# A decode block streamed through one core: 24 VectorE instructions joined or moved, and w2 loaded in four pieces

## The chip, the core and the metric

The kernel runs on one core of a Trainium2 chip. The core has TensorE (matrix products into PSUM), VectorE, ScalarE and GpSimd (elementwise work and reductions), and SyncE, which here issues every transfer between main memory (HBM) and SBUF. The five engines run their own instruction streams and wait for one another by semaphores. The metric is the device time of one execution in microseconds; lower is better.

## The reference

One token goes through a transformer block with adaptive layernorm. D is 640, there are 32 heads of 192, the cache holds 8192 positions, and the hidden layer has 1536. Everything is float32.

```python
mod = (silu(c) @ w_mod).reshape(1, 6, 1, 640)
sa, ca, ga, sb, cb, gb = (mod[:, i] for i in range(6))
h = layernorm(x) * (1 + ca) + sa
q = (h @ wq).reshape(1, 1, 32, 192).transpose(0, 2, 1, 3)
p = softmax(einsum("bhqd,bhkd->bhqk", q, k_cache) * 192 ** -0.5)
o = einsum("bhqk,bhkd->bhqd", p, v_cache)          # heads joined: 6144
x = x + ga * (o @ wo)
h = layernorm(x) * (1 + cb) + sb
r = maximum(h @ w1 + b1, 0)
x = x + gb * ((r * r) @ w2 + b2)
```

The caches are 201 MB each. Every byte of them is used once, so nearly all of the 452 MB that the kernel reads are cache.

## The kernel before

**The stream.** `plan()` cuts the work into 53 chunks. A chunk holds, for each of the 128 partitions, a row of key positions, a row of value units, and now and then a block of wq (for the next 512 columns of the query) or of wo (for the next pair of heads). A chunk has at most 16128 floats a partition, about 8 MB in all, and lies in one of three slots (`strm`, `slot`). SyncE issues `load(n + 3)` at the end of chunk n's part of the program; that transfer waits until every engine is through with the slot, and lies then in the queue behind what was issued before it. Behind the last chunk the same three slots take wm1 (the modulation weights for ga, sb, cb and gb), w1 and w2. The transfer of w2 is cut by `W2_CUT` into pieces, and each piece has a semaphore of its own. The products that read a piece wait for that piece. w2 has 12 blocks, each of 640 columns on 128 partitions (328 kB).

**The head of the program.** First comes wm0 (the weights for sa and ca, the first block of wq, x, c and the biases, in one transfer), and beside it wm0x, six small transfers into a part of the same slot that VectorE and GpSimd have filled with zeros. From these the program makes silu(c), the first two modulations, the first layernorm (`layernorm`, whose sums over partitions go through TensorE by `total`, a product with a tile of ones) and the first 512 columns of the query (`query`). Only then can VectorE begin on chunk 0.

**A chunk.** TensorE sums values weighted with p (`values`, line 331). VectorE multiplies the keys with the query (`multiply`, line 282). GpSimd adds the two halves of some of the products, and VectorE reduces the rest (`scores`, line 290). When a head's keys are through, `softmax` takes the maximum through a transpose on TensorE and lets ScalarE do the exponential. For each pair of heads `inverse` gives one over the sum on each partition, `evict` and `turn` bring the output of the heads into a column form (oT), and `attend` multiplies it by that pair's rows of wo, adding up in PSUM (att_a). The order of all this is the order of the code: there is no scheduler, and each engine runs its part in the order written.

**The tail.** After the last chunk the last pair is turned and attended, `mod` and `gate` make the last four modulations, `gather` brings the sum of the attention together, and the second layernorm gives h. The product with w1 goes to PSUM as ps_f. After it come two products into a bank that nobody reads (`ps_idle`). VectorE adds the bias, applies relu and the square, and transposes the result into fT. The product with w2 goes into ps_y, block by block (line 480), 4 matmuls a block, one for each quarter of the columns. VectorE multiplies by gb, adds x, and SyncE stores 640 floats.

The profile records a float32 matmul as two rows, so a block of w2 shows as 8 rows of TensorE.

Of the kernel before, what the change touches and what calls it, by code (L numbers as in the profile page):

```python
# [8 lines left out]
F32 = mybir.dt.float32  # L9
AF = mybir.ActivationFunctionType  # L10
ALU = mybir.AluOpType
AX = mybir.AxisListType

P = 128
D = 640
# [5 lines left out]
DG = D // G  # L21
FG = FF // G
KB = DG // 32
# [4 lines left out]
NV = DH // ED  # L28
# [17 lines left out]
LEAD_FROM = 1300  # L46
LEAD = 120
W1_CUT = (3 * FF, KB * FF)
W2_CUT = (6 * D, 10 * D, 12 * D)
WM_CUT = (KB * D + 9 * D, KB * D + 15 * D)  # L50
IDLE = 2
EPS = 1e-5
# [41 lines left out]
def block_kernel(ctx: ExitStack, tc: tile.TileContext, kv, wm0, wm0x, wm1, w1, w2, out):  # L94
    nc = tc.nc
    const = ctx.enter_context(tc.tile_pool(name="const", bufs=1))
# [5 lines left out]
    def slot(name):  # L102
        return strm.tile([P, SLOT], F32, tag="slot", name=name, bufs=3)
# [2 lines left out]
    ident = const.tile([P, P], F32, name="ident")  # L106
    make_identity(nc, ident)
    ones = const.tile([P, P], F32, name="ones")
    nc.vector.memset(ones, 1.0)

    mask = const.tile([P, E], F32, name="mask")
    nc.vector.tensor_reduce(mask, ident.rearrange("p (g e c) -> p e g c", g=G, e=E), axis=AX.XY, op=ALU.add)
    sel = const.tile([P, 1], F32, name="sel")
    nc.vector.tensor_reduce(sel, ident.rearrange("p (g c) -> p c g", g=G)[:, 0], axis=AX.X, op=ALU.add)
    eps_t = const.tile([P, 1], F32, name="eps_t")
    nc.vector.memset(eps_t, EPS)

    wm0_t = slot("wm0_t")
    wm0x_t = wm0_t[:64, SLOT - SX * WX:]
# [10 lines left out]
    x_c, c_c, bbc = small[:, :KB], small[:, KB:2 * KB + SX], small[:, 2 * KB + SX:]  # L130

    def columns(src, n, name, pool=const, **how):

        t = pool.tile([P, n // 32, 32], F32, name=name, **how)
        nc.vector.transpose(t.rearrange("p b r -> p (b r)"), src)
        return t
# [9 lines left out]
    def total(src, name):  # L146

        n = src.shape[1]
        ps = psum.tile([P, 512], F32, tag="sm", name="ps_" + name, bufs=2)
        nc.tensor.matmul(ps[:, :n], ones, src, start=True, stop=True)  # L150
        return ps[:, :n]

    def layernorm(x, copies, scale1, shift, name, between=lambda: None):

        n = x.shape[1]
        s = const.tile([P, 1], F32, name=name + "_s")
        nc.vector.tensor_reduce(s, x, axis=AX.X, op=ALU.add)
        m = const.tile([P, 1], F32, name=name + "_m")
        between()
        tm = total(s, name + "_tm")  # L160
        between()
        nc.vector.tensor_scalar(m, tm, 1.0 / (copies * D), None, op0=ALU.mult)
        xm = const.tile([P, n], F32, name=name + "_xm")
        nc.vector.tensor_scalar(xm, x, m, None, op0=ALU.subtract)
        sq = const.tile([P, n], F32, name=name + "_sq")
        ss = const.tile([P, 1], F32, name=name + "_ss")
        nc.vector.scalar_tensor_tensor(sq, xm, 1.0, xm, op0=ALU.mult, op1=ALU.mult, accum_out=ss)
        sd = const.tile([P, 1], F32, name=name + "_sd")
        nc.scalar.activation(sd, total(ss, name + "_tv"), AF.Sqrt, bias=eps_t, scale=1.0 / (copies * D))
        between()  # L170
        rs = const.tile([P, 1], F32, name=name + "_rs")
        nc.vector.reciprocal(rs, sd)
        h = const.tile([P, n], F32, name=name + "_h")
        nc.vector.scalar_tensor_tensor(h, xm, rs, scale1(), op0=ALU.mult, op1=ALU.mult)
        nc.vector.tensor_add(h, h, shift())
        return h


# [6 lines left out]
    mods = const.tile([P, 6, DG], F32, name="mods")  # L185
# [25 lines left out]
    def gate(m, w, steps):  # L211

        ps = psum.tile([P, 512], F32, tag="q", name=f"ps_mod{m}", bufs=2)
        b = 0
        for n in steps:
            for b in range(b, b + n):
                for k in range(2):
                    nc.tensor.matmul(ps[64 * k:64 * (k + 1), :2 * DG], e[:, b:b + 1].to_broadcast([P, 64]),
                                     w[:, b, 2 * DG * k:2 * DG * (k + 1)], start=(b == 0), stop=(b == KB - 1))
            b += 1  # L220
            yield
        for g in range(G):
            r = slice(32 * g, 32 * (g + 1))
            nc.scalar.activation(mods[r, m], ps[r, DG * (g % 2):DG * (g % 2 + 1)], AF.Copy)
        yield
# [4 lines left out]
    def load(n):  # L230
# [5 lines left out]
        else:  # L236
            name, src, cuts = (("wm1_t", wm1, WM_CUT), ("w1_t", w1, W1_CUT), ("w2_t", w2, W2_CUT))[n - len(PLAN)]
            chunk_t[name] = slot(name)
# [8 lines left out]
    load(1)  # L247
    mod(0, 2, wm0_t, wm0x_t)
    ma = columns(mods[:, 0:2].rearrange("p m n -> p (m n)"), 2 * DG, "ma")
    ca1 = const.tile([P, KB], F32, name="ca1")  # L250

    def scale_a():
        nc.vector.tensor_scalar(ca1, ma[:, KB:, 0], 1.0, None, op0=ALU.add)
        return ca1

    h1 = layernorm(x_c, 1, scale_a, lambda: ma[:, :KB, 0], "ln1")
    qb = const.tile([P, RING], F32, name="qb")

    def query(u, w):
        w = w.rearrange("p (b n) -> p b n", b=KB)  # L260
        ps = psum.tile([P, 512], F32, tag="q", name=f"ps_q{u}", bufs=2)
        for b in range(KB):
            nc.tensor.matmul(ps, h1[:, b:b + 1].to_broadcast([P, P]), w[:, b], start=(b == 0), stop=(b == KB - 1))  # L263
        nc.scalar.activation(qb[:, QC * u % RING:QC * u % RING + QC], ps, AF.Copy, scale=DH ** -0.5)  # L264


    att_a = psum.tile([P, 512], F32, tag="att", name="att_a")
    att_s = const.tile([P, D], F32, name="att_s")
    nc.vector.memset(att_s, 0.0)
    query(0, wm0_t[:, W0:W0 + WQ])  # L270

    sc = const.tile([P, SRING], F32, name="sc")
# [20 lines left out]
    ri_t, ps_t, sum_t = {}, {}, {}  # L293
# [57 lines left out]
    def turn(i):  # L351
        oT = work.tile([P, NV], F32, tag="oT", name=f"oT{i}")
        nc.vector.tensor_reduce(oT, os_t[i][:, :96].rearrange("p (j r) -> p j r", j=NV), axis=AX.X, op=ALU.add)  # L353
        nc.vector.tensor_scalar(oT, oT, ri_t.pop(i), None, op0=ALU.mult)  # L354
        os_t[i] = oT

    def attend(i, w):
        oT = os_t.pop(i)
        w = w.rearrange("p (j n) -> p j n", j=NV)
        first, last = i == 0, i == NPAIR - 1  # L360
        oW = work.tile([P, NV, 32], F32, tag="oW", name=f"oW{i}")
        nc.scalar.activation(oW, oT[:, :, None].to_broadcast([P, NV, 32]), AF.Copy)  # L362
        for j in range(NV):
            nc.tensor.matmul(att_a[96:, :512], oT[:, j:j + 1].to_broadcast([P, 32]), w[:, j, :512],  # L364
                             start=(first and j == 0), stop=(last and j == NV - 1))
        nc.tensor.matmul(att_a[:96, :NV * (D - 512)], oW.rearrange("p j r -> p (j r)"), w[:, :, 512:],  # L366
                         start=first, stop=last)
# [19 lines left out]
    for n, (kp, nk, vp, nv, extra) in enumerate(PLAN):  # L387
# [5 lines left out]
        for what, k in extra:  # L393
            w = t[:, at:at + EXTRA[what]]
# [10 lines left out]
        if nk:  # L405
            multiply(kt, kp, nk)
            m = nk - POOL * nk // 16
# [10 lines left out]
        for h in evicted:  # L418
            if h % 2:
                turn(h // 2)  # L420
# [11 lines left out]
        if wo_t is not None and n + 1 < len(PLAN):  # L432
            attend(*wo_t)
# [7 lines left out]
    for h in to_evict:  # L441
        evict(h)
    turn(NPAIR - 1)
    attend(*wo_t)
    mod(2, 3, wm1_t[:, KB * D:KB * 4 * D], between=gather)
    x1 = const.tile([P, DG], F32, name="x1")
    nc.vector.tensor_mul(x1, att_t[0][:, :DG], mods[:, 2])
    nc.vector.tensor_add(x1, x1, x_t)

    def scale_b():  # L450
        cb1 = const.tile([P, DG], F32, name="cb1")
        nc.vector.tensor_scalar(cb1, mods[:, 4], 1.0, None, op0=ALU.add)
        return cb1

    last = gate(5, gb_t, (2, 1, 2))
    hT2 = columns(layernorm(x1, 32, scale_b, lambda: mods[:, 3], "ln2", lambda: next(last)), DG, "hT2")
    next(last)

    pf = psum.tile([P, 512], F32, tag="q", name="ps_f", bufs=2)
# [6 lines left out]
        nc.tensor.matmul(idle, ones, w1_t[:, k, :512], start=True, stop=True)  # L466
    f = work.tile([P, FG], F32, name="f", tag="spread", bufs=1)
    nc.vector.tensor_add(f, pf[:, :FG], bbt[:, :FG])
    nc.vector.tensor_scalar(f, f, 0.0, None, op0=ALU.max)
    nc.vector.tensor_mul(f, f, f)  # L470
    fT = columns(f, FG, "fT", work, tag="om", bufs=1)

    gb2 = const.tile([P, DG], F32, name="gb2")
# [63 lines left out]
```

## Time and profile before

| | |
|---|---|
| median of three runs | 1055.33 us |
| lowest and highest | 1055.12, 1056.24 us |
| the profiled execution | 1055.26 us |
| its span, first to last instruction | 1053.5 us |
| HBM read | 451.83 MB |
| VectorE instructions, busy | 429, 831.5 us |
| ScalarE instructions, busy | 122, 43.5 us |
| GpSimd instructions, busy | 58, 189.7 us |
| mean granted TensorE clock | 0.723 of full speed |

The 1.8 us between the execution's time and its span lie around the first and the last instruction. Busy times of different engines overlap and don't add up to the span. In a group's row of the profile the columns are: line, engine, operation, output and inputs with their shape, count, then busy time in us and the mean of one in ns, then the idle time of the engine just before them and what ended it. A line of the chain has a start, a length and what ran. PE stands for TensorE and PEld for its weight load, DVE for VectorE, ACT for ScalarE, POOL for GpSimd, SP for SyncE.

### The profile page before, as it was taken

Reading aid. Unit: us, or ns where it says so; the run is one execution under the profiler, and the core shown is the slowest. Engines: PE = TensorE matmul, PEld = TensorE weight load, DVE = VectorE, ACT = ScalarE, POOL = GpSimd, SP = SyncE. Lnnn points to the kernel's source line nnn. Section 1 sums busy time; section 2 is a strip of 40 time slices with the busy share of each in tenths; the row PEclk is TensorE's granted clock in tenths of the full one; section 3 lists DMA queues with packets and bytes.
Section 4 is the critical chain, followed back from the end, with each engine's and each line's share of the span. In section 5 each row is a group of like instructions: output and inputs, shape, how many; then the busy total and the mean of one; then the engine's idle time right before and its main releaser. Section 6 shows DMA issues by size and latency. Waiting matters only on the chain.

```text
span 1053.5 us, 5195 instructions
## 1 busy us (share of the span) xinstructions
PE 495.3 (47%) x2130; PEld 135.0 (13%) x2130; DVE 831.5 (79%) x429; ACT 43.5 (4%) x122; POOL 189.7 (18%) x58
## 2 busy tenths in 40 slices
PE   3253344465352373435453366245346345445387
PEld 1010011011010010101010011001011011011023
DVE  1899878877959959888697895999888977988822
ACT  1000000000000000000000000000000000000001
POOL 0212121121212201212121121121211211212200
PEclk9676576778675686668667577676777767668689
DMA  9999999999999999999999999999999999999997
GB/s 408 427 432 443 437 438 436 428 430 429 434 436 431 432 431 435 436 430 437 430 427 431 434 445 436 431 427 433 431 432 437 431 434 434 434 436 431 420 426 317
DMA packets 8999, 452.15 MB, mean 429 GB/s; under 512 B 1016, under 2 KB 1020, under 8 KB 1148
## 3 DMA queue, kind: packets, MB, share of 16 engines
q1 hardware_dynamic: 8976, 451.83, 99.3%
q8 instruction: 16, 0.26, 0.1%
q14 instruction: 7, 0.06, 0.0%
HBM read 451.83 MB, written 0.00 MB: 429 GB/s over the span
## 4 chain that ended last, share of the span: by engine, by line
DMA 56%; DVE 31%; PE 11%; ACT 1%; issue 0%; SPq 0%; DVEq 0%
DMA chunk<-in_kv 53%; DVE chunk L282 16%; DVE sc L290 13%; PE ps_o L331 5%; PE att_a L364 2%; DMA w_t<-in_w 2%; PE ps_q L263 2%; DMA wm_t<-in_wm 1%; DVE os L345 1%; DVE om L343 1%; PE att_a L366 0%; ACT p L314 0%; PE ps_mx L306 0%; PE ps_mod L201 0%; PE ps_mod L207 0%
## 5 line engine op out<-in xcount | busy, mean ns | idle before, releaser
L282 DVE TENSOR_TENSOR chunk<-chunk,qb 128x8064 f32<-128x8064 f32 (+19 forms) x81 | 419.7, 5212 | 122.7 <-DMA chunk<-in_kv 118.0
L290 DVE TENSOR_REDUCE sc<-chunk 128x25 f32<-128x4800 f32 (+21 forms) x109 | 333.9, 3097 | 0.4
L409 POOL TENSOR_TENSOR chunk<-chunk 128x1824 f32<-128x1824 f32 (+9 forms) x51 | 187.4, 3674 | 803.8 <-DVE chunk L282 570.3
L331 PE MATMUL ps_o<-chunk,p 128*32 128x512 f32 x1536 | 292.3, 726 | 71.0 <-DMA chunk<-in_kv 61.5
L306 PE MATMUL ps_mx<-ident,mp 128*128 128x128 f32 x32 | 14.3, 447 | 346.4 <-DVE mp L304 346.4
L331 PEld LDWEIGHTS ps_o<-chunk,p 128*32 128x32 f32 x1536 | 66.6, 130 | 270.8 <-issue 184.0
L364 PE MATMUL att_a<-chunk,oT 128*32 128x512 f32 x96 | 68.1, 867 | 42.8 <-DVE oT L354 42.8
L263 PE MATMUL ps_q<-chunk,ln_h 128*128 128x512 f32 x110 | 65.8, 758 | 24.9 <-DMA chunk<-in_kv 24.9
L306 PEld LDWEIGHTS ps_mx<-ident,mp 128*128 128x128 f32 x32 | 5.6, 174 | 376.0 <-DVE mp L304 330.1
L314 ACT ACTIVATE p<-sc,nm 128x256 f32<-128x256 f32 x32 | 16.2, 507 | 648.5 <-DVE nm L308 648.5
L263 PEld LDWEIGHTS ps_q<-chunk,ln_h 128*128 128x128 f32 x110 | 26.4, 251 | 62.7 <-issue 34.5
L343 DVE TENSOR_TENSOR om<-ps_o,mask 96x512 f32<-96x512 f32 x32 | 21.6, 675 | 8.5 <-PE ps_o L331 8.5
L308 DVE TENSOR_REDUCE nm<-ps_mx 128x1 f32<-128x128 f32 x32 | 9.3, 292 | 19.9 <-PE ps_mx L306 19.9
L345 DVE TENSOR_REDUCE os<-om 96x64 f32<-96x512 f32 x32 | 21.8, 682 | 1.1
L364 PEld LDWEIGHTS att_a<-chunk,oT 128*32 128x32 f32 x96 | 12.4, 144 | 80.1 <-DVE oT L354 45.4
L353 DVE TENSOR_REDUCE oT<-ps_oT 128x3 f32<-128x96 f32 x16 | 4.0, 248 | 21.8 <-PE ps_oT L349 21.8
L319 PE MATMUL ps_sum<-ident,wide 128*128 128x128 f32 x16 | 7.5, 467 | 22.4 <-ACT wide L317 22.4
L349 PE MATMUL ps_oT<-ident,os 96*128 96x96 f32 x16 | 5.1, 321 | 25.8 <-DVE os L345 25.8
L201 PE MATMUL ps_mod<-wm_t,silu 128*32 128x480 f32 (+2 forms) x78 | 8.7, 584 | 14.4 <-DVE silu L183 14.4
L366 PE MATMUL att_a<-chunk,oW 128*96 128x384 f32 x32 | 14.8, 545 | 0.0
L264 ACT ACTIVATE qb<-ps_q 128x512 f32<-128x512 f32 x12 | 7.2, 597 | 135.4 <-PE ps_q L263 135.4
L362 ACT ACTIVATE oW<-oT 128x96 f32<-128x96 f32 x16 | 4.5, 280 | 176.5 <-DVE oT L354 176.5
(84 smaller groups left out, 104.8 us busy)
## 6 DMA issues: line engine op xcount, KB each, us to landing
chunk<-in_kv SPq DMA_DIRECT2D x38, 8064.0 KB, 35.1
chunk<-in_kv SPq DMA_DIRECT2D x11, 8000.0 KB, 37.2
chunk<-in_kv SPq DMA_DIRECT2D x2, 7872.0 KB
chunk<-in_kv SPq DMA_DIRECT2D x1, 6144.0 KB, 22.5
wm_t<-in_wm SPq DMA_DIRECT2D x1, 4480.0 KB
wm_t<-in_wm SPq DMA_DIRECT2D x1, 4257.0 KB, 12.5
chunk<-in_kv SPq DMA_DIRECT2D x1, 3264.0 KB
chunk<-in_kv SPq DMA_DIRECT2D x1, 3072.0 KB
```

Of the source, the lines that this page charges most:

```text
L263: nc.tensor.matmul(ps, h1[:, b:b + 1].to_broadcast([P, P]), w[:, b], start=(b == 0), stop=(b == KB - 1))
L282: nc.vector.tensor_mul(pr, pr, q[:, None, :].to_broadcast([P, b - a, DH]))
L290: nc.vector.tensor_reduce(sc[:, a % SRING:a % SRING + b - a], src[:, a - first:b - first], axis=AX.X, op=ALU.add)
L306: nc.tensor.transpose(ps[:, :P], mp.to_broadcast([P, P]), ident)
L308: nc.vector.tensor_reduce(nm, ps[:, :P], axis=AX.X, op=ALU.max, negate=True)
L314: nc.scalar.activation(p, s[:, :, None].to_broadcast([P, NPOS, 32 // E]), AF.Exp, bias=nm, accum_out=sp[:, h % 2:h % 2 + 1])
L331: nc.tensor.matmul(ps_t[h][32 * g:32 * (g + 1)], p[:, E * j:E * (j + 1)].rearrange("p e r -> p (e r)"), t[:, g], start=(j == 0), stop=last)
L343: nc.vector.tensor_mul(om[:n], ps_t.pop(h)[:n].rearrange("p (d e) -> p d e", e=E), mask[:n, None, :].to_broadcast([n, ED, E]))
L345: nc.vector.tensor_reduce(os_[:n, h % 2], om[:n], axis=AX.X, op=ALU.add)
L364: nc.tensor.matmul(att_a[96:, :512], oT[:, j:j + 1].to_broadcast([P, 32]), w[:, j, :512], start=(first and j == 0), stop=(last and j == NV ...
L366: nc.tensor.matmul(att_a[:96, :NV * (D - 512)], oW.rearrange("p j r -> p (j r)"), w[:, :, 512:], start=first, stop=last)
L409: nc.gpsimd.tensor_add(half, half, kt[:, m:, DH // 2:])
```

## The change

Five things are changed, and all values computed stay the same up to rounding.

1. In `turn` the multiplication of oT by one over the softmax sum is taken out (16 VectorE instructions, one for each pair). ScalarE's copy of oT into oW applies it as the copy's scale. The three wide products of `attend` read oW in place of oT, so they too now follow ScalarE's copy.
2. In `layernorm` the mean is no longer scaled by itself: one joined operation subtracts the scaled sum from x. The squares are written into h, which is overwritten later. The factor 1 + scale is multiplied into x minus the mean before the reciprocal of the root, and the last joined operation multiplies by that reciprocal and adds the shift. The instructions `ca1` and `cb1` are gone. Each of the two layernorms has two VectorE instructions fewer.
3. Relu and square are one joined operation.
4. `ones`, `eps_t` and `att_s` are filled by GpSimd in place of VectorE.
5. w2 comes in pieces of 6, 3, 2 and 1 block where it came in 6, 4 and 2.

```diff
-W2_CUT = (6 * D, 10 * D, 12 * D)
+W2_CUT = (6 * D, 9 * D, 11 * D, 12 * D)
...
-    nc.vector.memset(ones, 1.0)
+    nc.gpsimd.memset(ones, 1.0)
...
-    nc.vector.memset(eps_t, EPS)
+    nc.gpsimd.memset(eps_t, EPS)
...
-    def layernorm(x, copies, scale1, shift, name, between=lambda: None):
+    def layernorm(x, copies, scale, shift, name, between=lambda: None):
...
-        m = const.tile([P, 1], F32, name=name + "_m")
         between()
         tm = total(s, name + "_tm")
         between()
-        nc.vector.tensor_scalar(m, tm, 1.0 / (copies * D), None, op0=ALU.mult)
         xm = const.tile([P, n], F32, name=name + "_xm")
-        nc.vector.tensor_scalar(xm, x, m, None, op0=ALU.subtract)
-        sq = const.tile([P, n], F32, name=name + "_sq")
+        nc.vector.scalar_tensor_tensor(xm, tm.to_broadcast([P, n]), -1.0 / (copies * D), x, op0=ALU.mult, op1=ALU.add)
+        h = const.tile([P, n], F32, name=name + "_h")
         ss = const.tile([P, 1], F32, name=name + "_ss")
-        nc.vector.scalar_tensor_tensor(sq, xm, 1.0, xm, op0=ALU.mult, op1=ALU.mult, accum_out=ss)
+        nc.vector.scalar_tensor_tensor(h, xm, 1.0, xm, op0=ALU.mult, op1=ALU.mult, accum_out=ss)
         sd = const.tile([P, 1], F32, name=name + "_sd")
         nc.scalar.activation(sd, total(ss, name + "_tv"), AF.Sqrt, bias=eps_t, scale=1.0 / (copies * D))
         between()
+        nc.vector.scalar_tensor_tensor(xm, scale(), 1.0, xm, op0=ALU.add, op1=ALU.mult)
         rs = const.tile([P, 1], F32, name=name + "_rs")
         nc.vector.reciprocal(rs, sd)
-        h = const.tile([P, n], F32, name=name + "_h")
-        nc.vector.scalar_tensor_tensor(h, xm, rs, scale1(), op0=ALU.mult, op1=ALU.mult)
-        nc.vector.tensor_add(h, h, shift())
+        nc.vector.scalar_tensor_tensor(h, xm, rs, shift(), op0=ALU.mult, op1=ALU.add)
         return h
...
-    nc.vector.memset(att_s, 0.0)
+    nc.gpsimd.memset(att_s, 0.0)
...
-        nc.vector.tensor_scalar(oT, oT, ri_t.pop(i), None, op0=ALU.mult)
...
-        nc.scalar.activation(oW, oT[:, :, None].to_broadcast([P, NV, 32]), AF.Copy)
+        nc.scalar.activation(oW, oT[:, :, None].to_broadcast([P, NV, 32]), AF.Copy, scale=ri_t.pop(i))
         for j in range(NV):
-            nc.tensor.matmul(att_a[96:, :512], oT[:, j:j + 1].to_broadcast([P, 32]), w[:, j, :512],
+            nc.tensor.matmul(att_a[96:, :512], oW[:, j], w[:, j, :512],
                              start=(first and j == 0), stop=(last and j == NV - 1))
...
-    nc.vector.tensor_scalar(f, f, 0.0, None, op0=ALU.max)
-    nc.vector.tensor_mul(f, f, f)
+    nc.vector.scalar_tensor_tensor(f, f, 0.0, f, op0=ALU.max, op1=ALU.mult)
```

Three places show how the instructions stand before and after. In the rows, `x7` counts equal instructions, and the brackets name the engines or transfers whose semaphores an instruction waits for (DMAHW is a transfer's).

The first is ScalarE at the head of the program: silu, then the root of the first layernorm, then the first query and the table for the exponential. Before:

```order
L180 ACT_TABLE_LOAD
L180 ACTIVATE silu<-small 128x12 [waits DVE_49]
L169 ACT_TABLE_LOAD
L169 ACTIVATE ln_sd<-ps_ln_tv,eps_t 128x1 [waits PE_49]
L264 ACTIVATE qb<-ps_q_167 128x512 [waits PE_49]
L314 ACT_TABLE_LOAD
```

And now:

```order
L177 ACT_TABLE_LOAD
L177 ACTIVATE silu<-small 128x12 [waits DVE_49]
L167 ACT_TABLE_LOAD [waits PE_49]
L167 ACTIVATE ln_sd<-ps_ln_tv,eps_t 128x1 [waits Pool_49]
L255 ACTIVATE qb<-ps_q_162 128x512 [waits PE_49]
L305 ACT_TABLE_LOAD
```

The root now waits for GpSimd (eps_t) as well as for TensorE, and the wait for TensorE stands on the table load ahead of it.

The second is TensorE at the end of the program, where w1's product (ps_f), the two unread products and w2's product (ps_y) follow one another. Before:

```order
L462 MATMUL ps_f<-w_t,hT_2153 32x384 [waits DMAHW0_49]
L462 MATMUL ps_f<-w_t,hT_2153 32x384 x7
L466 MATMUL ps_idle<-w_t,ones 128x512 x2
L480 MATMUL ps_y<-w_t,fT 32x160 [waits DVE_49,DMAHW1_49,PE_49,Activation_49]
L480 MATMUL ps_y<-w_t,fT 32x160 x23
L480 MATMUL ps_y<-w_t,fT 32x160 [waits DMAHW2_49]
L480 MATMUL ps_y<-w_t,fT 32x160 x15
L480 MATMUL ps_y<-w_t,fT 32x160 [waits DMAHW3_49]
L480 MATMUL ps_y<-w_t,fT 32x160 x7
```

And now:

```order
L447 MATMUL ps_f<-w_t,hT_2128 32x384 [waits DMAHW0_49]
L447 MATMUL ps_f<-w_t,hT_2128 32x384 x7
L451 MATMUL ps_idle<-w_t,ones 128x512 [waits PE_49]
L451 MATMUL ps_idle<-w_t,ones 128x512
L464 MATMUL ps_y<-w_t,fT 32x160 [waits DVE_49,DMAHW1_49,PE_49,Activation_49]
L464 MATMUL ps_y<-w_t,fT 32x160 x23
L464 MATMUL ps_y<-w_t,fT 32x160 [waits DMAHW2_49]
L464 MATMUL ps_y<-w_t,fT 32x160 x11
L464 MATMUL ps_y<-w_t,fT 32x160 [waits DMAHW3_49]
L464 MATMUL ps_y<-w_t,fT 32x160 x7
L464 MATMUL ps_y<-w_t,fT 32x160 [waits DMAHW4_49]
L464 MATMUL ps_y<-w_t,fT 32x160 x3
```

Behind the last wait for a transfer stand 4 matmuls, where there were 8, and there is one such wait more.

The third is VectorE at the same place, from the second layernorm to fT. Before:

```order
L162 TENSOR_SCALAR ln_m<-ps_ln_tm 128x1 [waits PE_49]
L164 TENSOR_SCALAR ln_xm<-x_2117,ln_m 128x160 [waits DVE_49]
L167 SCALAR_TENSOR_TENSOR ln_sq,ln_ss<-ln_xm 128x160 [waits DVE_49]
L172 RECIPROCAL ln_rs<-ln_sd 128x1 [waits Activation_49]
L452 TENSOR_SCALAR cb_2149<-mods 128x160
L174 SCALAR_TENSOR_TENSOR ln_h<-ln_xm,ln_rs,cb_2149 128x160 [waits DVE_49]
L175 TENSOR_TENSOR ln_h<-ln_h,mods 128x160 [waits DVE_49]
L135 STREAM_TRANSPOSE hT_2153<-ln_h 128x160 [waits DVE_49]
L468 TENSOR_TENSOR f<-ps_f,bbt 128x384 [waits PE_49]
L469 TENSOR_SCALAR f<-f 128x384 [waits DVE_49]
L470 TENSOR_TENSOR f<-f 128x384 [waits DVE_49]
L135 STREAM_TRANSPOSE fT<-f 128x384 [waits DVE_49]
```

And now:

```order
L162 SCALAR_TENSOR_TENSOR ln_xm<-ps_ln_tm,x_2097 128x160 [waits PE_49]
L165 SCALAR_TENSOR_TENSOR ln_h,ln_ss<-ln_xm 128x160 [waits DVE_49]
L169 SCALAR_TENSOR_TENSOR ln_xm<-mods,ln_xm 128x160 [waits DVE_49]
L171 RECIPROCAL ln_rs<-ln_sd 128x1 [waits Activation_49]
L172 SCALAR_TENSOR_TENSOR ln_h<-ln_xm,ln_rs,mods 128x160 [waits DVE_49]
L135 STREAM_TRANSPOSE hT_2128<-ln_h 128x160 [waits DVE_49]
L453 TENSOR_TENSOR f<-ps_f,bbt 128x384 [waits PE_49]
L454 SCALAR_TENSOR_TENSOR f<-f 128x384 [waits DVE_49]
L135 STREAM_TRANSPOSE fT<-f 128x384 [waits DVE_49]
```

The product with 1 + scale (L169) now stands ahead of the instruction that waits for the root, and nine instructions stand where there were twelve.

More of the change, by code (lines that the diff above doesn't have):

```diff
@@ L249, in block_kernel @@
     ma = columns(mods[:, 0:2].rearrange("p m n -> p (m n)"), 2 * DG, "ma")
[L250 to L256, printed above, removed]
+    h1 = layernorm(x_c, 1, lambda: ma[:, KB:, 0], lambda: ma[:, :KB, 0], "ln1")
     qb = const.tile([P, RING], F32, name="qb")
@@ L448, in block_kernel @@
     nc.vector.tensor_add(x1, x1, x_t)
[L450 to L453, printed above, removed]
     last = gate(5, gb_t, (2, 1, 2))
-    hT2 = columns(layernorm(x1, 32, scale_b, lambda: mods[:, 3], "ln2", lambda: next(last)), DG, "hT2")
+    hT2 = columns(layernorm(x1, 32, lambda: mods[:, 4], lambda: mods[:, 3], "ln2", lambda: next(last)), DG, "hT2")
     next(last)
```

## The prediction

> **What bounds the kernel now.** I read the page first (shares, slices, queues, chain), then the chain of waits in order of time at both ends, then the timeline of the last 15 us, then the groups by line, and last the windows of half a microsecond for the granted clock.
>
> ```profile
> PE 495.3 (47%) x2130; PEld 135.0 (13%) x2130; DVE 831.5 (79%) x429; ACT 43.5 (4%) x122; POOL 189.7 (18%) x58
> DMA  9999999999999999999999999999999999999997
> q1 hardware_dynamic: 8976, 451.83, 99.3%
> HBM read 451.83 MB, written 0.00 MB: 429 GB/s over the span
> DMA 56%; DVE 31%; PE 11%; ACT 1%; issue 0%; SPq 0%; DVEq 0%
> L282 DVE TENSOR_TENSOR chunk<-chunk,qb 128x8064 f32<-128x8064 f32 (+19 forms) x81 | 419.7, 5212 | 122.7 <-DMA chunk<-in_kv 118.0
> chunk<-in_kv SPq DMA_DIRECT2D x38, 8064.0 KB, 35.1
> ```
>
> VectorE is busy 79% of the span and is named in 31% of the chain, which would make 24 fewer of its instructions look valuable. The other rows say no. The one queue of transfers is busy 99.3% of all 16 engines' time, no slice but the last is under 9 tenths, and VectorE's multiplies stood idle 118.0 us for chunks that had not landed. A typical chunk is 8064 KB, that is 8.26 MB. At the mean 429 GB/s it takes 19.2 us to move, but it lands 35.1 us after its issue. So it sat about 16 us behind the chunk ahead of it. The stream is fed early, and the VectorE pieces in the chain are only the last event before an issue that was itself early. The tightest early issue is chunk 3's:
>
> ```profile
> 0.74 12.50 DMA wm_t<-in_wm
> ...
> 46.97 10.22 DVE sc L290 x2
> ...
> 57.20 30.03 DMA chunk<-in_kv
> ```
>
> It still took 30.03 us, so 10.8 us of it was queueing. VectorE may be that much later there before the stream feels it. The stream itself begins at 0.74 us, with the first load, which waits for nothing.
>
> The end is the stream's end, and what follows it. The first rows are of the chain, the next of the timeline (start, length, and in brackets the idle time before and what ended it), the last of the transfers with their sizes:
>
> ```profile
> 1029.34 19.88 DMA w_t<-in_w
> ...
> 1049.26 0.80 PE ps_y L480 x16
> ...
> 1050.08 0.34 DVE y L483
> ...
> 1044.78 1.84 PE L480 MATMUL ps_y<-w_t,fT 128*32 128x160 f32 x48 [0.95 <-DVE x L475]
> 1047.75 1.29 PE L480 MATMUL ps_y<-w_t,fT 128*32 128x160 f32 x32 [1.13 <-DMA w_t<-in_w]
> 1049.26 0.75 PE L480 MATMUL ps_y<-w_t,fT 128*32 128x160 f32 x16 [0.22 <-DMA w_t<-in_w]
> ...
> w_t<-in_w SPq DMA_DIRECT2D x1, 1280.0 KB
> w_t<-in_w SPq DMA_DIRECT2D x1, 640.0 KB
> ```
>
> The last transfer of w2 was issued at about 1029.3 and landed at 1049.22. TensorE waited for the second and the third piece of w2 (1047.75, 1049.26), so the chain of small operations before it is not last. The third piece is 640 KB (655 KB in thousands) and landed 1.51 us after the second: 434 GB/s, the stream's own pace, 0.75 us a block.
>
> **The change, part by part.**
>
> *w2 in 6, 3, 2, 1 blocks.* This is the one part on the path. The 48, 32 and 16 records (two a matmul) took 1.84, 1.29 and 0.75 us, so eight matmuls more cost 0.55 and 0.54 us: 0.068 us each, over some 0.2 us that every group pays. After the last landing now come 4 matmuls in place of 8: 4 x 0.068 = 0.27 us less. The two-block piece lands at about 1049.22 - 0.75 = 1048.47, and its 0.75 us are over as the last block lands; if it is late by a little, it eats part of the gain. The path gains 0.27 us.
>
> One transfer is added, with 128 packets of 2560 bytes, 8 for each engine. SP issues it at about 1029.7, some 19 us ahead of need. The trace has no packet of that size. From below, the 640 KB piece with 5120-byte packets ran at 434 GB/s, so nothing: 0. From above, the same trace's smallest transfer, the output:
>
> ```profile
> 1052.00:1052.50 0.50, 0.00 (x0) 0.00 (x0) 0.00 (x0) 0.00 (x0) 0.00 (x0) 1.00 0.02 5
> out_y<-y SPq DMA_DIRECT2D x1, 2.5 KB
> ```
>
> A share of 0.02 (0.025 at most) of 16 engines in half a microsecond is 0.2 us for its 4 packets, 0.05 us each, where 640 bytes at 27 GB/s need 0.024: at most 0.03 us extra a packet, 0.2 us for eight. I take 0, since the 5120-byte packets are nearest in size; 0.2 stays for the range. A gain is excluded: the bytes are the same.
>
> The two landings 1.51 us apart leave no room for a time of its own between queued transfers. The Trainium skill, "DMA: Bandwidth & Descriptors", section "Anatomy of one DMA — SWDGE (gpsimd) path", gives each transfer a fixed cost of about 2.0 us beside its bytes, measured on GpSimd's path; by it, if paid in turn, the sum would be -0.27 + 2.0 = +1.7 us.
>
> *The 16 multiplications by the inverse sum (L354).*
>
> ```profile
> L354 DVE TENSOR_SCALAR oT<-oT,r 128x3 f32<-128x3 f32 x16 | 3.7, 228 | 0.6
> L362 ACT ACTIVATE oW<-oT 128x96 f32<-128x96 f32 x16 | 4.5, 280 | 176.5 <-DVE oT L354 176.5
> ```
>
> VectorE is relieved of 16 x 0.228 = 3.7 us (4.1 with the handover). All of it lies in front of waits for chunks, the last pair's in front of w1 and w2: worth 0. For each pair TensorE's three wide products now read ScalarE's copy, so they wait 0.280 us for it where they waited 0.228 for L354: about 0.05 us later, unless the per-partition scale makes the copy dearer (a copy with a scale and one without are not side by side in the trace; anything up to doubling it stays under 0.4 us). Behind them in TensorE's queue are the products with values, and SP's issue of a later chunk waits for the pair's last product: 0.4 us against 10.8 us of queueing. Worth 0.
>
> *The first layernorm.* On its path one VectorE instruction goes ahead of the sum of squares and two behind the root. But ScalarE's root now needs eps_t from GpSimd as well as TensorE's sum; the wait for TensorE stands on the table load ahead of it.
>
> ```profile
> 13.71 1.28 ACT L169 ACT_TABLE_LOAD   x1
> 24.21 0.16 DVE L162 TENSOR_SCALAR ln_m<-ps_ln_tm 128x1 f32<-128x1 f32 x1 [0.47 <-PE ps_ln_tm L150]
> 25.52 0.26 ACT L169 ACTIVATE ln_sd<-ps_ln_tv,eps_t 128x1 f32<-128x1 f32 x1 [10.53 <-PE ps_ln_tv L150]
> 26.34 0.17 DVE L175 TENSOR_TENSOR ln_h<-ln_h,ma 128x5 f32<-128x5 f32 x1
> 33.97 12.96 DVE L282 TENSOR_TENSOR chunk<-chunk,qb 128x12288 f32<-128x12288 f32 x1 [4.70 <-ACT qb L264]
> ```
>
> Before, the load ran at 13.71, long before the root at 25.52. Now it starts at about 25.3: +1.28 us. The joined instructions give back 0.19 (L162 and its handover), 0.19 (the scale of 1 + ca) and 0.26 (L175): 0.64. The query, and with it the first multiply, comes 0.6 us later, at about 34.6. Chunk 3 is issued at 57.8 in place of 57.2, out of 10.8 us of queueing. Worth 0; if the cover were gone, +0.6.
>
> *Memsets to GpSimd.* The two of ones and eps now stand ahead of wm0x's memset on GpSimd, some 0.3 us by its own 128x128 memset (0.20). SP's six small loads and chunk 0 wait for that one, 3.3 to 3.6; they queue behind the first load, which lands at 13.24. The third, att_s, is needed at 1028. GpSimd's first real work is at 47. Worth 0.
>
> *The second layernorm and relu-square.* At about 1035 to 1044, L162 and its handover (0.20) against a costlier joined subtraction, 1 + cb and L175 (0.26 and 0.36) against a product done while the root is awaited, and L469 (0.36 and its handover, 0.39) go: about 1.1 us.
>
> ```profile
> L469 DVE TENSOR_SCALAR f<-f 128x384 f32<-128x384 f32 x1 | 0.4, 360 | 0.0
> L452 DVE TENSOR_SCALAR cb<-mods 128x160 f32<-128x160 f32 x1 | 0.2, 224 | 0.0
> L175 DVE TENSOR_TENSOR ln_h<-ln_h,mods 128x160 f32<-128x160 f32 x1 | 0.3, 325 | 0.0
> L480 PEldq EVENT_SEMAPHORE  x2: 51/51/51, 1044.2 to 1044.7; - x2
> 1043.56 0.58 DVE L135 STREAM_TRANSPOSE fT<-f 128x384 f32<-128x384 f32 x1
> ```
>
> fT was ready at 1044.14, and TensorE's second wait ended at 1044.7: that is w2's first piece (four blocks at 0.75 us ahead of 1047.75 agree). Being 1.1 us earlier only lengthens that wait. Worth 0.
>
> **Sum.** On the profiled execution: 1055.26 - 0.27 + 0 = 1055.0 us (1053.5 of it span, 1.8 around it). The median of the runs before is 1055.33, 0.07 above that execution, so this is also 0.3 us under the median.
>
> **The rivals.**
>
> *The VectorE chain counts.* If the 31% were true limits, all removed work would show: 4.1 us of L354, 1.1 us in the tail, 0.27: 1049.8. For it: the chain's share. Against it: 118.0 us of waiting for chunks, 99.3% on the queue.
>
> *TensorE's clock falls at the end (slower).* With fT up to 1.1 us earlier, TensorE rests longer before w2's first piece. The columns here are the stretch, its length, the busy time of PE, PEld, DVE, ACT and POOL, the granted clock, the share of the transfer engines and GB/s.
>
> ```profile
> 1020.80:1024.20 3.40, 1.27 (x4) 0.47 (x5) 1.84 (x4) 0.28 (x1) 0.00 (x0) 1.00 0.89 381
> 1024.50:1027.50 3.00, 3.00 (x5) 0.35 (x3) 0.00 (x0) 0.00 (x0) 0.00 (x0) 0.50 1.05 441
> 1041.30:1044.70 3.40, 2.53 (x12) 0.68 (x4) 2.58 (x6) 0.00 (x0) 0.00 (x0) 1.00 0.97 401
> ```
>
> After 3.4 us in which TensorE was busy 37%, the granted clock was 0.50 for the next 3 us, although TensorE worked all through them. A stretch of 74% (1041.30 on) kept 1.00. With the change that last stretch holds at most 0.6 us less work: 1.9 of 3.4, 56%, between the two. If the clock falls at 1044.7 and stays down to the end, 48 matmuls at twice 0.068 and the 0.2 take until 1044.75 + 6.7 = 1051.5, where 1049.26 + 0.80 = 1050.06 was: +1.4, or 1056.7 us. It decides from the point where that stretch comes near 37%. The Trainium skill, "TensorE: Matmul & The Clock Gate", section "HAM oscillation — how this bites in real kernels", has the rule that the array must not rest more than about 3.4 us on end. By it a wait of 1.4 us is harmless. The trace's fall, after a stretch that was busy for 37%, is stricter than that rule, so I leave the rival a chance.
>
> *The added transfer costs a time of its own (slower).* A lone small transfer does: the output's was issued from 1050.79 for 0.60 us, and the span ends at 1053.5, 2.1 us behind that.
>
> ```profile
> 1050.79 0.60 SPq L485 DMA_DIRECT2D out_y<-y  x1
> ```
>
> If the fourth piece paid that in turn, behind the third, the end would be 1055.0 + 2.1 = 1057.1. Against it: two queued pieces 1.51 us apart at full pace. The page named above would give 2.0 for the 2.1; the landings here don't bear it out for queued transfers.
>
> *The stream runs slower.* The end hangs on 451.83 MB at 429 GB/s; the three runs before lay from 1055.12 to 1056.24, so one in three stood 0.9 us above the median with nothing changed. That gives 1056.1; twice that excess is 1057.1.
>
> *The change does not do what it says.* The instruction order shows that it does, with the table load's wait as the one thing unsaid: +0.6 us if it counted, 1055.6.
>
> **How the numbers follow.** Forecast 1055.0, by about a microsecond to each side: 0.72. A slower stream: 0.13. The clock: 0.05. The added transfer's own time: 0.03. The table load or another small wait of the head that comes through: 0.02. The VectorE chain: 0.05. A measurement of this kernel can tell about 0.2% from no change, 2.1 us: below 1053.2 or above 1057.4. Faster by more has the VectorE chain alone, 0.05. Slower by more has the far end of the stream's scatter, and a little of the clock and the added transfer on top of it: 0.07. Within it: 0.88. The range starts a microsecond under the forecast, since the scatter seen has only gone up, and ends where the clock rival and most of the stream's scatter lie: 1054.0 to 1056.9.
>
> **What would show it.** Right: the last group of TensorE's L464 starts as w2's last piece lands and is over some 0.5 us later in place of 0.80; SP's issues, the queue's 99% and the landing of w2 stay where they are; VectorE has about 5 us less busy time and as much more waiting for chunks; the first multiply starts at 34 to 35 us, after a table load at about 25. Wrong: VectorE's wait for chunks stays at 118 us while the span shrinks; a granted clock of 0.50 after 1044; the last piece of w2 landing more than 0.2 us later than 1049.2; a slice of the queue under 9 tenths.

## The result, and the profile after

The changed kernel takes 1052.56 us (median; 1052.38 to 1053.07), where the kernel before takes 1055.33 (1055.12 to 1056.38). The ratio is 0.9972, with a 95% interval from 0.9962 to 0.9982. So it is faster by 0.28%, 2.8 us, ten times what the prediction had for it.

The page of the changed kernel, in the rows that answer to those quoted of before (busy time of the engines, the transfer queue with packets, MB and share of 16 engines, the chain, and VectorE's multiplies with the time they waited for chunks):

```profile
PE 486.7 (46%) x2130; PEld 133.8 (13%) x2130; DVE 826.2 (79%) x405; ACT 44.9 (4%) x122; POOL 190.5 (18%) x61
q1 hardware_dynamic: 9120, 451.83, 99.4%
HBM read 451.83 MB, written 0.00 MB: 430 GB/s over the span
DMA 56%; DVE 30%; PE 12%; ACT 1%; issue 0%; SPq 0%; DVEq 0%; ACTq 0%
L273 DVE TENSOR_TENSOR chunk<-chunk,qb 128x8064 f32<-128x8064 f32 (+19 forms) x81 | 419.6, 5211 | 126.7 <-DMA chunk<-in_kv 121.5
```

VectorE lost 5.3 us of work, and its wait for chunks grew from 118.0 to 121.5 us although the span is 2.9 us shorter. That is what work off the path looks like when it is removed. The queue is as full as before, but it now moves the same 451.83 MB at 430 GB/s in place of 429.

The chain at the end of the changed kernel (start, length, what):

```profile
1027.31 18.61 DMA w_t<-in_w
1045.92 0.04 issue
1045.97 0.75 PE ps_y L464 x16
1046.72 0.03 issue
1046.75 0.52 PE ps_y L464 x8
1047.27 0.02 issue
1047.30 0.34 DVE y L467
```

VectorE's last product starts at 1047.30 where it was 1050.08: 2.78 us earlier. The two blocks before the last one landed at 1045.92, and the last block was there when their matmuls were through. The landing moved. Before, all of w2 had landed at 1049.22; now by 1046.75 at the latest. So some 2.5 us of the 2.8 lie ahead of the last matmuls, in the stream.

Where in the stream? Two of VectorE's multiplies that a landing released, near the start and near the end of the chunks, show it. First the kernel before:

```profile
106.31 2.16 DVE L282 TENSOR_TENSOR chunk<-chunk,qb 128x1920 f32<-128x1920 f32 x1 [1.38 <-DMA chunk<-in_kv]
962.87 4.56 DVE L282 TENSOR_TENSOR chunk<-chunk,qb 128x4224 f32<-128x4224 f32 x1 [4.44 <-DMA chunk<-in_kv]
```

And the changed one:

```profile
106.45 2.16 DVE L273 TENSOR_TENSOR chunk<-chunk,qb 128x1920 f32<-128x1920 f32 x1 [1.41 <-DMA chunk<-in_kv]
961.14 9.03 DVE L273 TENSOR_TENSOR chunk<-chunk,qb 128x4224 f32<-128x4224 f32 x2 [4.69 <-DMA chunk<-in_kv]
```

At 106 the changed kernel is 0.14 us late, at 962 it is 1.73 us early. Between the two lie 45 chunks: 856.56 / 45 = 19.035 us a chunk before, 854.69 / 45 = 18.993 now. Each chunk comes 0.042 us sooner on average, 0.22%. The other multiplies that waited for a chunk show it too (0.05 us early at 201, 0.64 at 411, 1.11 at 601, 1.48 at 811). Some 0.2 us of it is a single step between the multiplies at 315 and 392 us; over the 9 chunks ahead of that step and the 30 behind it the slope is even, 0.037 and 0.038 us a chunk. The removed instructions can hardly be read into that. The 16 products by the inverse sum come once in three chunks, and in no slice of the span but the last is the queue under 9 tenths busy.

### The profile page after: what moved, and what is told of

It is laid out like the page before. It is cut to its first block, busy times and chain, and to the rows that moved or that the text cites. A ratio compares the mean times of both kernels' runs of the same rounds, so it can differ in the third digit from the quotient of the medians.

```text
span 1050.6 us, 5178 instructions
## 1 busy us (share of the span) xinstructions
PE 486.7 (46%) x2130; PEld 133.8 (13%) x2130; DVE 826.2 (79%) x405; ACT 44.9 (4%) x122; POOL 190.5 (18%) x61
## 3 DMA queue, kind: packets, MB, share of 16 engines
q1 hardware_dynamic: 9120, 451.83, 99.4%
HBM read 451.83 MB, written 0.00 MB: 430 GB/s over the span
## 4 chain that ended last, share of the span: by engine, by line
DMA 56%; DVE 30%; PE 12%; ACT 1%; issue 0%; SPq 0%; DVEq 0%; ACTq 0%
DMA chunk<-in_kv 53%; DVE chunk L273 16%; DVE sc L281 12%; PE ps_o L322 6%; PE ps_q L254 2%; PE att_a L354 2%; DMA w_t<-in_w 2%; DMA wm_t<-in_wm 1%; DVE os L336 1%; DVE om L334 1%; PE att_a L356 0%; ACT p L305 0%; PE ps_mx L297 0%; PE ps_mod L198 0%; PE ps_mod L204 0%
## 5 line engine op out<-in xcount | busy, mean ns | idle before, releaser
L273 DVE TENSOR_TENSOR chunk<-chunk,qb 128x8064 f32<-128x8064 f32 (+19 forms) x81 | 419.6, 5211 | 126.7 <-DMA chunk<-in_kv 121.5
L322 PE MATMUL ps_o<-chunk,p 128*32 128x512 f32 x1536 | 287.1, 716 | 68.8 <-DMA chunk<-in_kv 59.4
L354 PE MATMUL att_a<-chunk,oW 128*32 128x512 f32 x96 | 64.2, 824 | 44.9 <-ACT oW L352 44.9
L354 PEld LDWEIGHTS att_a<-chunk,oW 128*32 128x32 f32 x96 | 12.1, 141 | 81.3 <-ACT oW L352 47.6
L352 ACT ACTIVATE oW<-oT,r 128x96 f32<-128x96 f32 x16 | 5.9, 372 | 174.6 <-DVE oT L344 174.6
```

The source lines that it names most:

```text
L273: nc.vector.tensor_mul(pr, pr, q[:, None, :].to_broadcast([P, b - a, DH]))
L322: nc.tensor.matmul(ps_t[h][32 * g:32 * (g + 1)], p[:, E * j:E * (j + 1)].rearrange("p e r -> p (e r)"), t[:, g], start=(j == 0), stop=last)
L354: nc.tensor.matmul(att_a[96:, :512], oW[:, j], w[:, j, :512], start=(first and j == 0), stop=(last and j == NV - 1))
```

## What else the change moves

The diff has one more effect, which none of its lines names. The pool of constants lies ahead of the three slots in SBUF, and the change drops six tiles from it: `ca1`, `cb1`, and a mean and a square for each layernorm. The addresses in the two built programs, in bytes within a partition:

```
                         before            after
constants end, slot a    26752 = 104.5 x 256    25344 = 99 x 256
slot b                   91264 = 356.5 x 256    89856 = 351 x 256
slot c                  155776 = 608.5 x 256   154368 = 603 x 256
```

1408 bytes fewer, and the slots, which were 128 bytes past a multiple of 256, lie on one. Each is 64512 bytes long, 252 x 256, so all three share that place. A chunk's transfer writes one row into each of 128 partitions, 8 rows for each of 16 engines.

**Theory A:** a row that starts off a multiple of 256 bytes in SBUF costs its transfer engine a fixed little more. Before, 62 transfers wrote 128 rows each (54 of chunks, wm0, and 7 of the tail), 62 x 8 = 496 rows an engine; 2.2 us over 496 rows is 4.4 ns a row, and 8 rows of a chunk 0.035 us, near the 0.037 and 0.038 above. **Theory B:** the edits themselves let the stream run faster, by less traffic on SBUF or by slots that come free sooner.

## The experiments

All were timed beside the kernel before, which had medians of 1055.39, 1055.47 and 1055.39 us in the three groups of runs. Differences below are against the median of the same group. An unused tile can move the slots without touching anything that runs. The spans given in this section, from first to last instruction, are medians over a kernel's executions; they scatter less than the times.

**The slots moved, the instructions left alone.**

```diff
     y = const.tile([P, DG], F32, name="y")
+    const.tile([P, 32], F32, name="pad")
```

> The kernel before with one unused tile of 128 bytes a partition put last into the constants, so that the three slots start at 26880, a multiple of 256 bytes, where they started at 26752 (128 past one). Nothing else changes. Theory A (a transfer's row that starts off a multiple of 256 bytes in SBUF costs a little more on its engine): the stream's pace gets 0.2% faster, the chunks drift to 1.7 us earlier by 980, time 1053.0 us. Theory B (the changed instructions let the stream run faster, by less traffic on SBUF or earlier slots): 1055.3, no drift.

1053.14 us (1052.90 to 1053.96), ratio 0.9978 (0.9969 to 0.9988): 2.25 us less with the instructions of the kernel before. (The small work tiles, which lie behind the slots, move by the same 128 bytes.) Its chunks:

```profile
106.37 2.16 DVE L282 TENSOR_TENSOR chunk<-chunk,qb 128x1920 f32<-128x1920 f32 x1 [0.86 <-DMA chunk<-in_kv]
961.33 9.03 DVE L282 TENSOR_TENSOR chunk<-chunk,qb 128x4224 f32<-128x4224 f32 x2 [4.41 <-DMA chunk<-in_kv]
```

854.96 / 45 = 18.999 us a chunk, near the 18.993 of the changed kernel. Theory B has no place for this.

**The changed kernel, moved off again**, by 128, 64 and 192 bytes, with the small work tiles kept in their place within 512 bytes. The edit for 128 bytes is shown; for 64 and 192 the two tiles have 16 and 112, and 48 and 80 floats:

```diff
+    work.tile([P, 96], F32, name="wpad", tag="wpad", bufs=1)
     x_t = spread(x_c, KB, "x_t")
...
     y = const.tile([P, DG], F32, name="y")
+    const.tile([P, 32], F32, name="pad")
```

> The changed kernel with 128 unused bytes ahead of the slots, so that they start 128 past a multiple of 256 again, and 384 behind them, so that the small work tiles keep their place within 512 bytes. Theory A: the stream is as slow as before, the gain of the last w2 piece alone is left: 1054.9 us. Theory B: 1052.6.

> The same with 64 bytes (slots 64 past a multiple of 256). Theory A with a cost that grows with the bytes between the multiple and the start: half of the 2.3 us, 1053.7. Theory A with one and the same cost for every start off the multiple: 1054.9. Theory A with a grain of 64 bytes, not 256: 1052.6. Theory B: 1052.6.

> The same with 192 bytes (slots 192 past a multiple of 256). Growing cost: 1056.1. One cost for all: 1054.9. Grain of 64 bytes, or theory B: 1052.6.

1054.63, 1054.76 and 1054.71 us. All three lose 2.1 to 2.2 us against the changed kernel, and the distance from the multiple makes no difference: not half of it at 64, not half as much again at 192. The multiply at 962.87 of before starts at 963.04 in the one with 128:

```profile
963.04 4.56 DVE L273 TENSOR_TENSOR chunk<-chunk,qb 128x4224 f32<-128x4224 f32 x1 [4.71 <-DMA chunk<-in_kv]
```

So a start on a multiple of 64 or of 128 doesn't do, and the three starts off 256 cost the same within 0.13 us. The Trainium skill, "DMA: Bandwidth & Descriptors", section "How a descriptor splits into AXI transactions", says that a descriptor (here one row) starting on a multiple of 256 bytes is cut into transactions of 256, and one starting elsewhere begins with a partly used transaction from the multiple below, whose unused bytes cost beats of 32 bytes too. It gives no time for this and names no side, source or target. An estimate from its beats has the cost grow with the distance, 2, 4 and 6 beats for 64, 128 and 192. The runs agree with the grain of 256 bytes, but not with such a growth: 1054.76, 1054.63 and 1054.71 us. One transaction more a row, whatever is unused in it, would fit the three equal times; no run shows the transactions themselves.

**A control: the slots moved by 256 bytes.**

```diff
+    work.tile([P, 64], F32, name="wpad", tag="wpad", bufs=1)
     x_t = spread(x_c, KB, "x_t")
...
     y = const.tile([P, DG], F32, name="y")
+    const.tile([P, 64], F32, name="pad")
```

> The changed kernel with 256 unused bytes ahead of the slots and 256 behind them: the slots move as in the other padded kernels, but stay on a multiple of 256 (now of 512 too). If only the distance to a multiple of 256 counts: 1052.6 us. If 512 is the grain, a further gain of about 2: 1050.5. If any move of the slots by padding costs: 1054.7.

1052.68 us (1052.55 to 1053.01), ratio 0.9973 (0.9963 to 0.9983). Padding as such costs nothing, and a multiple of 512 gives nothing beyond one of 256.

**Is it a cost for each row, or for the bytes?** Each chunk but the last loaded in two halves doubles its rows and leaves the bytes:

```diff
-            cuts = (m,) if n + 1 < len(PLAN) else ((PLAN[n][3] + 1) // 2 * UNIT, m)
+            cuts = (m // 128 * 64, m) if n + 1 < len(PLAN) else ((PLAN[n][3] + 1) // 2 * UNIT, m)
```

> The changed kernel with each chunk but the last loaded in two halves, by columns, so that every partition's row becomes two rows, each starting on a multiple of 256 bytes in SBUF and in HBM. If a row that starts on the multiple costs nothing of its own: 1052.6 us. It serves as the base of the next run.

> The same halves with the slots 128 bytes past a multiple of 256: each engine now has 114 x 8 rows that start off the multiple, where the unsplit kernel has 62 x 8. If the cost is one for each row (4.2 ns a row, from 2.07 us over 496 rows): 3.8 us above the aligned halves, 1056.4. If the cost goes with the bytes (every piece of a row lies across a boundary): 2.1 above the aligned halves, 1054.7. If the slots' place matters by something else than the start of rows: no forecast, but no reason for more than 2.1.

1055.36 us on the multiple (1055.25 to 1056.64), 1059.45 off it (1059.13 to 1059.48; its ratio to the kernel before is 1.0035, 1.0022 to 1.0047). The difference is 4.09 us, near twice the 2.07 of the undivided rows. The changed kernel has one transfer more than the kernel before, so it is 63 x 8 = 504 rows on an engine that gave 2.07 us, 4.1 ns a row, and 115 x 8 = 920 that gave 4.09, 4.4 ns a row. The cost goes with the number of rows that start off the multiple, not with the bytes. I had expected the aligned halves to be free, and they were not: 52 more transfers, with 52 x 8 = 416 more rows an engine, cost 2.80 us, though the queue was as full:

```profile
q1 hardware_dynamic: 16608, 451.84, 99.5%
```

Some 0.4 us of the 2.80 lies outside the span: the spans are 1053.2 us with the halves and 1050.8 without, 2.4 us apart, or 0.046 us for each added transfer. The traces have the same: the multiply at 277.29 of the changed kernel comes 0.44 us later with the halves, the one at 979.73, 37 chunks on, 2.14 us, again 0.046 us a chunk. Whether the rows bear that (it would be 5.8 ns each) or the transfer itself isn't shown, since both grew together. The packets grew from 9120 to 16608, by 144 for each added transfer: its 128 rows and 16 more.

So one more transfer of 128 rows cost about 0.05 us on the full queue, and each row that starts off a multiple of 256 some 4 ns on its engine.

**Does the place in HBM count as well?** 32 floats ahead of the chunks move every row's source by 128 bytes.

```diff
-    start = [sum(width(c) for c in PLAN[:n]) * P for n in range(len(PLAN))]
+    start = [32 + sum(width(c) for c in PLAN[:n]) * P for n in range(len(PLAN))]
...
-        "kv": np.concatenate(kv),
+        "kv": np.concatenate([np.zeros(32, np.float32)] + kv),
```

> The changed kernel with 32 unused floats ahead of the chunks in HBM, so that every chunk's rows start 128 bytes later in HBM, while the slots stay on a multiple of 256 in SBUF. If the place in HBM costs as the place in SBUF did (2.07 us for 62 rows a partition, here 54 of them): 1054.4 us. If only the place in SBUF counts: 1052.6.

> Both: rows start 128 bytes past a multiple of 256 in SBUF and 128 bytes later in HBM. If what costs is a source and a target that are not alike to each other within 256 bytes: 1052.9 us, since they are alike again (but for the rows of the tail). If each place costs by itself: 1056.4. If SBUF's alone counts: 1054.6.

1052.74 (1052.47 to 1053.02) and 1054.76 us (1054.40 to 1055.64). The source's place costs nothing that can be seen, with the slots on the multiple or off it. What counts is the place in SBUF, not a difference between source and target. The traces don't give the arrays' addresses in HBM, so whether the rows lay on a multiple of 256 there before they were moved stays open.

**The cut of w2 by itself**, in the kernel before and, the other way round, taken out of the changed one:

```diff
-W2_CUT = (6 * D, 10 * D, 12 * D)
+W2_CUT = (6 * D, 9 * D, 11 * D, 12 * D)
```

> The kernel before with w2 in 6, 3, 2 and 1 block and nothing else changed; the slots stay 128 bytes past a multiple of 256. If the cut is worth what the prediction made of it (4 matmuls fewer behind the last landing, the landing where it was): 1055.1 us. If the cut also brings the last landing forward: 1054.7, with the VectorE edits then worth nothing. If the cut is worth nothing: 1055.4.

> The changed kernel with w2 in 6, 4 and 2 blocks as before; the slots stay on a multiple of 256. By the prediction's term: 0.27 us more than the changed kernel, 1052.8. If the cut also brings the last landing forward: 1053.1, as the kernel before with moved slots. If the VectorE edits are what the moved slots don't explain: 1052.6.

1055.08 us, 0.39 less than the kernel before of its group, with a ratio that leaves no change possible (0.9988 to 1.0005); and 1053.28 (1052.86 to 1054.37), 2.19 less and above all three forecasts. The second leaves 2.77 - 2.19 = 0.58 us for the cut, but across two groups, and its runs are spread over 1.5 us. More of its time also lies outside the span, 2.28 us at the median, where the changed kernel has 1.80. The spans put the cut at 0.3 us in the first (1053.2 against 1053.5) and 0.4 in the second (1050.8 against 1051.2). The traces are finer. Here is TensorE's w2 in the kernel before with the new cut:

```profile
1044.70 1.84 PE L480 MATMUL ps_y<-w_t,fT 128*32 128x160 f32 x48 [1.13 <-DMA w_t<-in_w]
1046.91 1.02 PE L480 MATMUL ps_y<-w_t,fT 128*32 128x160 f32 x24 [0.38 <-DMA w_t<-in_w]
1048.45 1.26 PE L480 MATMUL ps_y<-w_t,fT 128*32 128x160 f32 x24 [0.52 <-DMA w_t<-in_w]
1049.78 0.33 DVE L483 TENSOR_TENSOR y<-ps_y,mods 128x160 f32<-128x160 f32 x1 [5.34 <-PE ps_y L480]
```

and in the changed kernel with the old cut:

```profile
1046.75 0.75 PE L464 MATMUL ps_y<-w_t,fT 128*32 128x160 f32 x16 [0.23 <-DMA w_t<-in_w]
1047.56 0.33 DVE L467 TENSOR_TENSOR y<-ps_y,mods 128x160 f32<-128x160 f32 x1 [6.07 <-PE ps_y L464]
```

The last product on VectorE starts 0.30 us earlier for the cut in the first (1050.08 before), 0.26 in the second (1047.30 in the changed kernel). Part of this is how far the stream had come. Counted from the start of w2's first group, VectorE's product comes after 5.08 us in the first, where the kernel before has 5.30 (from 1044.78); in the second it comes after 5.29 us (from 1042.27), where the changed kernel has 5.07 (from 1042.23). By that the cut is worth 0.22 us both times. In the first the last three blocks run through without a wait: the single block was there when the two before it were multiplied.

The second kernel has all the VectorE edits and the aligned slots, but not the cut. At 2.19 us it stands where the kernel before with moved slots stands (2.25; the spans are 1051.2 and 1051.3). So with the slots on the multiple the edits of VectorE, ScalarE and GpSimd by themselves are worth 0 within 0.1 us or so. Off the multiple the same comparison leaves more: the changed kernel with 128 bytes is 0.76 us below its kernel before, the cut alone 0.39. The other 0.37 is more than scatter between the two groups: the spans are 1052.8 (1052.6 to 1053.0) and 1053.2 (1053.1 to 1053.4), and the kernel before has 1053.5 in both groups. It lies in the stream and not in VectorE's tail, as w2's first group starts at 1044.39 in the one trace and at 1044.70 in the other. The small work tiles lie otherwise in these two kernels, 256 and 128 bytes past a multiple of 512 in the built programs; no run moved them alone, and the cause of the 0.37 stays open.

**The table load at the head**, with eps_t on VectorE again:

```diff
-    nc.gpsimd.memset(eps_t, EPS)
+    nc.vector.memset(eps_t, EPS)
```

> The changed kernel with eps_t filled by VectorE as before; ScalarE's table load for the root then waits for nothing and runs early again, and the first multiply comes some 1.3 us sooner, at about 33.5. If the head is covered by the queue, as the prediction has it: 1052.6 us. If the later start counts: 1051.4.

1052.64 us (1052.50 to 1052.77), no difference to the changed kernel. The head is covered. The first multiply was only a little sooner than in the changed kernel, though, at 34.64 and not at the expected 33.5. ScalarE and VectorE there, first in the changed kernel:

```profile
25.58 1.28 ACT L167 ACT_TABLE_LOAD   x1 [11.90 <-PE ps_ln_tv L150]
26.87 0.26 ACT L167 ACTIVATE ln_sd<-ps_ln_tv,eps_t 128x1 f32<-128x1 f32 x1
34.17 0.60 ACT L255 ACTIVATE qb<-ps_q 128x512 f32<-128x512 f32 x1 [7.04 <-PE ps_q L254]
34.80 12.96 DVE L273 TENSOR_TENSOR chunk<-chunk,qb 128x12288 f32<-128x12288 f32 x1 [5.07 <-ACT qb L255]
```

and then with the early load:

```profile
25.72 0.26 ACT L167 ACTIVATE ln_sd<-ps_ln_tv,eps_t 128x1 f32<-128x1 f32 x1 [10.79 <-PE ps_ln_tv L150]
34.01 0.60 ACT L255 ACTIVATE qb<-ps_q 128x512 f32<-128x512 f32 x1 [8.03 <-PE ps_q L254]
34.64 12.96 DVE L273 TENSOR_TENSOR chunk<-chunk,qb 128x12288 f32<-128x12288 f32 x1 [6.06 <-ACT qb L255]
```

The root came 1.15 us earlier and the query only 0.16: ScalarE waited 8.03 us for TensorE's query in place of 7.04. TensorE began the query's products 1.16 us earlier (26.49, 27.65) and took 7.48 us for them in place of 6.49. The granted clock accounts for that. It was 0.50 as they began in both traces and then 1.00. From 31 to 32 us its mean was 0.72 in the changed kernel, and from 32 to 33 us 0.80 with the early load, after a full 0.50 in the microsecond before; so it rose at about 31.56 and 32.40. The products ran 3.9 us at half clock in the one and 5.9 in the other, and 2.0 us more at half clock make up the 1.0 us.

## Why the prediction was wrong

**The bound was read rightly.** The stream sets the end, and work taken from VectorE only lengthens its waits. The moved slots alone, with the old instructions, gave 2.25 us; the edits without the cut, no more than about 0.1 beside that (off the multiple up to 0.4, unexplained).

**The step that failed is the sum's "+ 0" for all but w2's cut.** The prediction had every part on the path priced through instructions and waits, and took the stream's pace as given: "the queue's 99% and the landing of w2 stay where they are". Its only reason was, for the added transfer, that "the bytes are the same". The landing of w2 moved by some 2.5 us. The pace was a term. It was 2.0 us in the changed kernel (2.77 us under the kernel before, where the one moved off by 128 is 0.76 under its own) and 2.25 in the kernel before. What set it was in the program, not in the profile: the dropped tiles are in the diff, and the slots come behind them. A slower stream was among the rivals, but as scatter of one and the same kernel, and a faster one was not. None of the prediction's signs of being wrong came, since none of them stood for a faster stream. (In the line of the sum, 1053.5 and 1.8 us are the parts of 1055.26, not of 1055.0.)

**The queue's share could not show it.** It was 99.3% before and 99.4% after. A busy engine is not an engine at its best pace. What showed it were the starts of the multiplies, which drifted apart by 0.042 us a chunk.

**The cut of w2** was put at 0.27 us. Its size was right: the traces have 0.22 us from the start of w2's products and 0.30 and 0.26 at their end, the spans 0.3 and 0.4. The way there was a little different. The last wait that counted was the one for the two-block piece, at 1045.92 in the changed kernel, and 12 matmuls stood behind it. The single block was there by 1046.75, as the two before it were through; when it landed the rows don't show.

**The added transfer's own time** was bounded between 0 and 0.2 us. In the kernel with halves a transfer more cost about 0.05 us; the one in w2, with its rows of 2560 bytes, was not measured by itself. The rival that it would be paid in turn at about 2 us falls: the kernel before with the new cut took 1055.08 us against 1055.47.

**The inverse sum in ScalarE's copy**: worth 0, as forecast. The copy got dearer with its scale, as was left open:

```profile
L352 ACT ACTIVATE oW<-oT,r 128x96 f32<-128x96 f32 x16 | 5.9, 372 | 174.6 <-DVE oT L344 174.6
```

372 ns in place of 280. TensorE now waits these 372 ns where it waited 228 for VectorE's product, some 0.14 us more for each pair, under the cover that the prediction named.

**The head**: the load started at 25.58 (forecast 25.3) and the first multiply at 34.80 (34.6). Chunk 3, issued at 58.03, landed after 29.30 us at 87.33; it was 87.23 before. Covered, as forecast.

**TensorE's clock at the end** kept 1.00 until TensorE was through, in every stretch from 1041 to 1048 us. The VectorE chain as a limit falls with the kernels that kept the edits and lost the gain.

## What to carry to other kernels

A kernel that lives on one stream of transfers can have part of its pace in where the buffers lie, and any tile that is added or dropped ahead of them moves them. Look up the addresses of the streamed buffers in the built program, before and after, and put them on a multiple of 256 bytes by an unused tile: here that is one line for 0.2%. Count transfers too: each one added to the full queue here, with its 128 rows, cost about 0.05 us.

When a change is timed faster, compare landings early and late in the stream before crediting its instructions. A gain that grows evenly from the first chunk to the last belongs to the stream.

## What was not expected of the hardware

A row that starts off a multiple of 256 bytes in SBUF costs 4.1 to 4.5 ns more on its engine (2.25 us over 496 rows, 2.07 over 504, 4.09 over 920), the same for 64, 128 and 192 bytes. A start moved by 128 bytes in HBM costs nothing that could be told. A transfer with rows of some 64 kB that is cut into two with half rows costs about 0.05 us more, even with rows that start on the multiple and a queue that is 99.5% busy. And 1.15 us taken from the wait ahead of TensorE's first query gave only 0.16 us at its end, because TensorE then ran 2.0 us longer at a granted clock of 0.50.
